# Who issues a V shift, where a q turn stands in SyncE's queue, and when the next chunk's k and q are loaded

## The chip, the cores and the metric

The kernel runs on one core of a Trainium2 chip. The metric is the device time of one execution in microseconds. The other figures come from one profiled execution; its span runs from its first to its last instruction.

## The reference, cut to what matters

Attention over 4 batches of 8 heads, 768 positions and 64 features per head: three heads (0, 2, 6) are causal, the other five see the first 4 keys and a window of 64. Then two dense layers with a leaky ReLU between.

```python
scores = (1 / sqrt(D)) * q @ k.transpose(0, 1, 3, 2)
mask   = causal (heads 0, 2, 6)  or  causal & (pos_k < 4 | rel < 64) (heads 1, 3, 4, 5, 7)
a      = softmax(where(mask, scores, -1e9))
x      = (a @ v).transpose(0, 2, 1, 3).reshape(3072, 512)
h      = x @ w_in                    # 512 -> 2048
out    = maximum(0.01 * h, h) @ w_out   # 2048 -> 512
```

## The kernel before, in words

The 3072 rows are cut into eight chunks of 384: chunk n is half c of batch b, and each batch has two chunks. All matmuls are bf16 with float32 sums. Every chunk goes through the same stations, and the kernel works at three chunks at a time. Its order is written out by hand: in the loop at L1154 round n does the first layer of chunk n (`in_slots`, letter t), the attention of chunk n + 1 (letter a), the second layer of earlier tiles (letter p) and the spreading of chunk n + 2's keys (letter e), and the string `WOVEN[n]` says letter by letter which of these pieces is issued next. Each engine then runs its own instructions strictly in the order of issue.

The stations of one chunk, with the names that the trace uses:

- **Loads**, issued by GpSimd: `load_qk` (L110, the DMA at L116) brings k into `kb` and q into `qb`, three transfers each; there is one buffer of each. `load_v` (L118, L123) brings V into `va`, three transfers. With `behind`, a one-element copy into `hold` (L121) first makes GpSimd wait for a given tile.
- **Turns**, issued by SyncE: `turn_dma` (L245, L254) transposes `kb` into `kd` and `qb` into `qd` by DMA.
- **Spread**: VectorE copies `kd` into the key tiles `kt` (L274). It can't begin before the k turn has landed.
- **V shift**: `v_shift` (L146; L150, L151) copies V, moved by 64 rows, from `va` into `vb` in two DMAs, by SyncE if no other engine is given. The window heads read `vb` as an operand of TensorE's second attention product (L336).
- **Attention** (L316): scores on TensorE (L368, L404), exponentials on ScalarE (L373, L409), masks on VectorE (L376, L378, L413), the product with V (L336). `finish` (L427) divides a pair of heads by its sums into `xs` (L438, VectorE), and `x_t` (L441) has SyncE turn `xs` into a quarter of `xt` by DMA (L443). A chunk has four such outputs, one for each pair.
- **First layer**: TensorE multiplies `w_in_bf` with `xt` (L622, one bank `ph` of two for each piece, emptied by ScalarE at L625 into `g_all`), and for some columns by a scheme with seven products in the place of eight (L710), which needs sums of `xt` from VectorE (`x_sum`, L662).
- **Second layer**: seven products for a pair of row tiles (L834), with sums of `g_all` (L793); results are stored by SyncE (L868).

What sets the order around the change is round n = 2 of the loop. It has the attention of chunk 3, whose four outputs SyncE turns. At its head it turns k and q of chunk 4 (L1160) and has GpSimd load k and q of chunk 5 (L1167); ScalarE issues the V shift of chunk 4 at the letter v (L1174). The rounds 3 and 4 end with a copy into `hold` that waits for the last quarter of the next chunk's `xt` (L1185), and behind it GpSimd loads q and V for later chunks. Round 3 begins with the turns of chunk 5 and the load of its V behind its k turn (L1162).

A DMA's queue is that of the engine that issues it. SyncE, GpSimd and ScalarE each issue in order, and an instruction that waits holds up all that stand behind it on its engine.

Of the kernel before, what the change touches and what calls it, by code (L numbers as in the profile page):

```python
# [21 lines left out]
def kernel(  # L22
# [12 lines left out]
    nc = tc.nc  # L35
# [10 lines left out]
    NCH = B * (S // CH)  # L46
# [63 lines left out]
    def load_qk(n, nms="kq"):  # L110
        b, c = ORDER[n]
        for nm in nms:
            t = rot.tile([128, 3, H, D], BF16, name=f"{nm}b", tag=f"{nm}b", bufs=1)
            raw[nm, n] = t
            for g in range(3):
                nc.gpsimd.dma_start(out=t[:, g], in_=nat[nm][b, c, :, :, g])  # L116

    def load_v(n, gs=range(3), behind=None):  # L118
        b, c = ORDER[n]
        if behind is not None:  # L120
            nc.gpsimd.tensor_copy(hold[0:1, :], behind)  # L121
        for g in gs:
            nc.gpsimd.dma_start(out=va[b][:, 3 * c + g, :, 0:D], in_=nat["v"][b, c, :, :, g])  # L123
# [3 lines left out]
    def load_sinks(b, eng=None):  # L127
        vsf[b] = vsfs[b % 2]
        (eng or nc.sync).dma_start(out=vsf[b].rearrange("(r f) d -> r f d", f=4)[:, 0], in_=v[b, :, 0:NS, :])

    def sink_values(b, eng):
        n = H - 1
        eng.tensor_tensor(
            vs[b % 2][:, 1:H, 0:D],
            vsf[b].rearrange("p (o d) -> p o d", o=1).to_broadcast([128, n, D]),
            m_sink[:, 1:H].rearrange("p (h o) -> p h o", o=1).to_broadcast([128, n, D]),
            op=ALU.mult)
# [8 lines left out]
    def v_shift(n, eng=None):  # L146
        eng = eng or nc.sync
        i, c = ORDER[n]
        lo, hi = (0, 2) if c == 0 else (2, 5)
        eng.dma_start(out=vb[i][0:64, lo:hi], in_=va[i][64:128, lo:hi, 1:H])  # L150
        eng.dma_start(out=vb[i][64:128, lo:hi], in_=va[i][0:64, lo + 1 : hi + 1, 1:H])  # L151
# [64 lines left out]
    def turn_pair(n, p, tags, engs, nms="kq"):  # L216
        b, c = ORDER[n]
        prepared.update((nm, n, p) for nm in nms)
        if n not in qx:
            qx[n] = rot.tile([128, 4, CH], BF16, name="qt", tag="qd", bufs=3)  # L220
        for nm, tag, eng in zip(nms, tags, engs):
            pt = bank(tag, [128, 4, 128], BF16)
            for g in range(3):
                nc.tensor.transpose(pt[:, g, :], raw[nm, n][:, g, 2 * p : 2 * p + 2, :], ident[:])
            if nm == "k":
                for hh in range(2):
                    move(eng[hh], kt[b % 2][hh][:, p, CH * c : CH * c + CH].rearrange("p (g t) -> p g t", g=3), pt[:, 0:3, :], hh)
            else:
                move(eng, qx[n][:, p, :].rearrange("p (g t) -> p g t", g=3), pt[:, 0:3, :])
# [15 lines left out]
    def turn_dma(n, nms="kq"):  # L245
        for nm in nms:
            dst = rot.tile([128, 3, 4, 128], BF16, name=f"{nm}d", tag=f"{nm}d", bufs=3 if nm == "q" else 2)
            if nm == "q":
                qx[n] = dst
            else:  # L250
                raw["kx", n] = dst
            thirds = [slice(j, j + 1) for j in range(1 if nm == "q" and n == 3 else 3)]
            for g in thirds if n < 4 or (nm, n) == ("k", 4) else [slice(0, 3)]:
                nc.sync.dma_start_transpose(out=dst[:, g].rearrange("p g q t -> p (g q) t"),  # L254
                                            in_=raw[nm, n][:, g].rearrange("p g h d -> p (g h d)"))
# [8 lines left out]
    def spreads(n):  # L264
        b, c = ORDER[n]

        def spread(g, hh):
            r = slice(64 * hh, 64 * hh + 64)
            o = CH * c + 128 * g
            dst, src = kt[b % 2][hh][r, :, o : o + 128], raw["kx", n][r, g]  # L270
            if n == 2 and hh:
                nc.scalar.activation(out=dst, in_=src, func=ACTF.Copy)
            else:
                nc.vector.tensor_copy(dst, src)  # L274

        order = [(g, hh) for hh in range(2) for g in range(3)] if n < 4 else [(g, hh) for g in range(3) for hh in range(2)]
        r = [lambda g=g, hh=hh: spread(g, hh) for g, hh in order]
        if c == 0:
            r += sink_keys_by(b)
        return r  # L280
# [210 lines left out]
    class First:  # L491
# [108 lines left out]
    RAMP = "XXqqqqaxYaYaaXaYakakakaaZaaZkaZsaasaaasaaataattaaatatattat"  # L600
    FIRST = "tttttttDttttL0tttt10Wt0kkk4k10k00k1k1S000k00S00aav011aSa22aa1Sa1a11a1aT1a11aa22a2a2eeaea2ee2eaa"
    WOVEN = {
        2: "aaptpIataatataatataIataItaattIaaetaeapeaatatvateaaepetteppe",
        3: "aappapapaxAppptAAaaAAtpAatAaaptaaBBAptpeeBaapaBBvetpBBpetetBe",
        4: "paappapapaxppaaApaatapatAaapAapAaAtpAaAeaeBpteeapapetaaABpeptpaBpBepatBptBpevBppppBpp",
        5: "paaxAteaAeatpaaAAtpIAaappaABApaatpBppeatBaeAIppaIeBBptpBItBtpBev",
# [139 lines left out]
    def in_tile(t0, j, tag="ph", nt=4):  # L746
        ph = bank(tag, [128, 4, 128], FP32)
        for x in range(nt):
            t = t0 + x
            for g in range(KG):  # L750
                nc.tensor.matmul(ph[:, x, :], lhsT=w_in_bf[:, g, 128 * t : 128 * t + 128],  # L751
                                 rhs=xts[0][:, j, g, :], start=(x == 0 and g == 0),
                                 stop=(g == KG - 1), skip_group_check=True)
        done[0] += nt / 3
        nc.scalar.activation(out=g_all[:, slab(0) + j, t0 : t0 + nt, :], in_=ph[:, 0:nt], func=ACTF.Prelu, alpha=0.01)
# [171 lines left out]
    def steps(k, units=None):  # L927

        r = []
        for u in units or Pair.UNITS[pairs[k].duo]:  # L930
            for half in range(2):
                def step(u=u, half=half):
                    pairs[k].unit(u, half)
                    if not half:
                        return flush()
                    pending.extend((pairs[t], i) for t, i in sums_behind(k, u))
                    flush()
                r.append(costing(0.44, step))
        return r
# [77 lines left out]
    for a in (ats4[0], ats[0]):  # L1017
# [63 lines left out]
    lists = {  # L1081
        "x": [lambda: F2.x_t("py", "v")],
        "X": [lambda j=j: in_tile(0, j) for j in range(3)],
        "Y": [lambda j=j: in_tile(4, j, nt=2) for j in range(3)],
        "Z": [lambda j=j: in_tile(6, j, nt=2) for j in range(3)],
        "q": [
            lambda: turn_pair(1, 0, ("ph",), ('v',), "q"),
            lambda: turn_pair(1, 1, ("po",), ('v',), "q"),
            lambda: turn_pair(1, 3, ("psS",), ('a',), "q"),
# [37 lines left out]
    def turn_third():  # L1127
# [3 lines left out]
    lists = {  # L1131
        "t": p1,
        "0": steps(0, ("P1", "P2", "P6", "P7", "P5", "P4", "P3")),
        "1": steps(1, ("P1", "P2", "P6", "P7", "P5", "P4", "P3")),
        "2": steps(2),
        "W": [behind_first],
        "4": [lambda: then_fourth.pop()()],
        "S": [lambda i=i: pairs[1].sum(i) for i in range(1, 5)],
        "k": keys2,
# [14 lines left out]
    for n in range(2, NCH):  # L1154
        a, extra = [], []
        if n + 2 < NCH:
            if ORDER[n + 2][1] == 0:
                load_sinks(ORDER[n + 2][0])
                sink_values(ORDER[n + 2][0], nc.gpsimd)
            turn_dma(n + 2, "q" if n == 5 else "kq")  # L1160
            if n == 3:
                load_v(n + 2, behind=raw["kx", n + 2][0:1, 0, 0, 0:1])  # L1162
            if n == 4:
                v_shift(n + 2)
            extra = spreads(n + 2)
            if n + 3 < NCH:
                load_qk(n + 3, "k" if n > 2 else "kq")  # L1167
        if n + 1 < NCH:
            a = Attention(n + 1, cross=True).slots(lag=2 if n > 3 else 3)
        lists = {"a": a, "p": outs, "x": [lambda: x_sums(n)], "e": extra, "v": [], **in_slots(n)}  # L1170
        if n in (3, 5):
            lists["v"] = [lambda: v_shift(n + 2)]
        if n == 2:
            lists["v"] = [lambda: v_shift(4, nc.scalar)]  # L1174
        if n == 4:
            lists["v"] = [lambda: turn_dma(7, "k")]
        if n in (5, 6):
            lists["I"] = in_sums_left
        if n == 2:
            lists["I"] = [lambda i=i: in_sums(0, i + 1) for i in range(4)]  # L1180
        for c in WOVEN[n]:
            lists[c].pop(0)()
        assert not any(lists[c] for c in lists if c not in "xI") and (n < 6 or not in_sums_left)
        if n in (3, 4):
            nc.gpsimd.tensor_copy(hold[0:1, :], xts[n + 1][0:1, 3, 0:1])  # L1185
            load_qk(n + 3, "q")
            load_v(n + 3)
        outs = [f for k in range(3 * n // 2, 3 * n // 2 + 1 + n % 2) for f in steps(k)]
    run(outs)

# [34 lines left out]
```

## Time and profile before

| | us |
|---|---|
| median of 3 runs | 220.78 |
| the three runs | 218.86, 220.78, 221.34 |
| the profiled execution | 219.31 |
| its span, first to last instruction | 217.4 |
| TensorE busy | 209.0 (96%) |
| VectorE busy | 165.3 (76%) |
| ScalarE busy | 150.3 (69%) |
| GpSimd busy | 72.5 (33%) |

The engines are named PE (TensorE), DVE (VectorE), ACT (ScalarE), POOL (GpSimd) and SP (SyncE). A name with a q behind it, as SPq, is the engine's issuing part: a row of it is the issue of a DMA, not its transfer. An arrow inside a name reads as "written from" (xt<-xs); behind a wait it names what ended the wait. TensorE's clock is granted in full in all 40 slices of the page.

### The profile page before, as it was taken

The numbers are of one execution on the slowest core, as the hardware profiler recorded it, in microseconds if no ns is written. First come the engines' busy times: TensorE is split into PE (matmuls) and PEld (weight loads), VectorE is DVE, ScalarE is ACT, GpSimd is POOL, SyncE is SP. The second block draws the span as 40 slices with busy tenths as digits, with TensorE's granted clock in tenths as the row PEclk, the third lists the DMA queues.
The fourth block names the chain that finished last, engine by engine and source line by source line (L and its number), as shares of the span: only waits on it lengthen the run. The fifth ranks groups of instructions, "written<-read, shape, count | busy, mean of one in ns | idle before, by whom it ended". The sixth has DMA issues, their size and how long they took to land.

```text
span 217.4 us, 6311 instructions
## 1 busy us (share of the span) xinstructions
PE 209.0 (96%) x2524; PEld 174.2 (80%) x2524; DVE 165.3 (76%) x454; ACT 150.3 (69%) x348; POOL 72.5 (33%) x91
## 2 busy tenths in 40 slices
PE   7798999999999999989999999999999999999994
PEld 5577887568898677778887978788888999999893
DVE  6683596897699477868886875799997986977653
ACT  4766985766566896658679876686677995668420
POOL 8977563019805913607219500900000000000000
PEclk9999999999999999999999999999999999999999
DMA  9999999999999999999999995996140131200222
GB/s 131 148 174 171 184 207 192 172 157 123 167 135 197 205 134 151 161 230 135 139 171 202 123 139 144 174 167 100 50 138 3 21 106 48 101 0 0 100 97 96
DMA packets 112604, 28.79 MB, mean 132 GB/s; under 512 B 102208, under 2 KB 109632, under 8 KB 112576
## 3 DMA queue, kind: packets, MB, share of 16 engines
q0 software_dynamic: 78080, 13.37, 85.4%
q1 hardware_dynamic: 33152, 14.53, 35.3%
q10 hardware_dynamic: 1344, 0.50, 1.1%
q8 instruction: 19, 0.31, 0.6%
q14 instruction: 9, 0.07, 0.1%
HBM read 27.30 MB, written 6.29 MB: 154 GB/s over the span
## 4 chain that ended last, share of the span: by engine, by line
PE 84%; DMA 7%; POOL 5%; ACTq 1%; ACT 1%; DVE 1%; issue 1%; POOLq 0%
PE py L834 18%; PE ph L622 16%; PE ph L710 9%; PE po L336 7%; PE py L813 7%; PE psS L368 5%; PE po L710 5%; DMA w_in_bf<-in_moe_w_in_dram 4%; DMA xt<-xs 3%; PE psS L404 3%; PE psS L622 2%; PE po L813 2%; PE ph L751 2%; PE po L834 2%; PE ph L813 1%; PE psS L710 1%
## 5 line engine op out<-in xcount | busy, mean ns | idle before, releaser
L622 PE MATMUL ph<-xt,w_in_bf 128*128 128x384 bf16 x224 | 44.6, 326 | 1.3 <-DMA xt<-xs 0.7
L625 ACT ACTIVATE g_all<-ph 128x384 bf16<-128x384 f32 x56 | 27.3, 490 | 16.8 <-PE ph L622 15.8
L373 ACT ACTIVATE at<-psS 128x384 bf16<-128x384 f32 x73 | 33.9, 493 | 6.5 <-PE psS L368 5.9
L622 PEld LDWEIGHTS <-w_in_bf 128*128 128x128 bf16 x256 | 23.4, 98 | 12.0 <-issue 0.8
L834 PEld LDWEIGHTS <-sum 128*128 128x128 bf16 x256 | 23.9, 98 | 2.5
L116 POOL DMA_DIRECT2D kb<-in_k_dram x21 | 18.8, 921 | 18.5 <-DMA kd<-kb 17.3
L123 POOL DMA_DIRECT2D va<-in_v_dram x24 | 21.4, 916 | 1.9 <-DMA qb<-in_q_dram 1.5
L834 PEld LDWEIGHTS <-g_all 128*128 128x128 bf16 x192 | 17.9, 98 | 2.9 <-issue 0.2
L116 POOL DMA_DIRECT2D qb<-in_q_dram x21 | 18.6, 906 | 3.8 <-DMA w_in_bf<-in_moe_w_in_dram 1.6
L368 PE MATMUL psS<-qd,kt 128*128 128x384 bf16 (+2 forms) x81 | 19.1, 290 | 0.0
L336 PE MATMUL po<-va,at 128*128 128x65 bf16 x219 | 18.5, 194 | 0.0
L409 ACT ACTIVATE ats<-psS 128x384 bf16<-128x384 f32 x33 | 15.7, 490 | 2.6 <-PE psS L404 2.4
L793 DVE TENSOR_TENSOR sum<-g_all 128x1024 bf16<-128x1024 bf16 x24 | 16.4, 683 | 1.2 <-ACT g_all L625 0.9
L336 PEld LDWEIGHTS <-at 128*128 128x128 bf16 x234 | 14.5, 98 | 3.4 <-issue 0.7
L834 PE MATMUL py<-w_sum,sum 128*128 128x256 bf16 x120 | 17.2, 272 | 0.0
L834 PE MATMUL py<-w_out_bf,sum 128*128 128x256 bf16 x120 | 16.7, 273 | 0.0
L738 ACT ACTIVATE s<-ph 128x384 f32<-128x384 f32 x27 | 13.1, 491 | 5.1 <-PE ph L710 4.5
L834 PE MATMUL py<-w_out_bf,g_all 128*128 128x256 bf16 x112 | 16.1, 273 | 0.0
L438 DVE TENSOR_TENSOR xs<-po,linv 128x384 bf16<-128x384 f32 x27 | 15.0, 557 | 0.9
L413 DVE TENSOR_TENSOR ats<-ats,m_win 128x384 bf16<-128x384 bf16 x35 | 12.2, 354 | 4.3 <-ACT ats L409 3.9
L710 PEld LDWEIGHTS <-w_in_bf 128*128 128x128 bf16 x168 | 14.1, 98 | 1.7 <-issue 1.1
L729 DVE TENSOR_TENSOR s<-po,s 128x384 f32<-128x384 f32 x21 | 11.4, 554 | 3.8 <-ACT s L738 1.8
(248 smaller groups left out, 497.5 us busy)
## 6 DMA issues: line engine op xcount, KB each, us to landing
out_dram<-o SPq DMA_DIRECT2D x23, 256.0 KB, 2.8
va<-in_v_dram POOLq DMA_DIRECT2D x24, 128.0 KB, 6.3
qb<-in_q_dram POOLq DMA_DIRECT2D x21, 128.0 KB, 7.2
kb<-in_k_dram POOLq DMA_DIRECT2D x21, 128.0 KB, 6.5
w_out_bf<-in_moe_w_out_dram POOLq DMA_DIRECT2D x4, 512.0 KB, 11.9
w_in_bf<-in_moe_w_in_dram POOLq DMA_DIRECT2D x2, 512.0 KB, 8.6
w_in_bf<-in_moe_w_in_dram POOLq DMA_DIRECT2D x4, 256.0 KB, 8.2
vb<-va SPq DMA_DIRECT2D x6, 170.6 KB, 4.0
```

The source lines that it names most:

```text
L116: nc.gpsimd.dma_start(out=t[:, g], in_=nat[nm][b, c, :, :, g])
L123: nc.gpsimd.dma_start(out=va[b][:, 3 * c + g, :, 0:D], in_=nat["v"][b, c, :, :, g])
L336: nc.tensor.matmul(o, lhsT=lhsT, rhs=rhs, start=first, stop=False, skip_group_check=True)
L368: nc.tensor.matmul(s[:, off : off + w], lhsT=kt[i][hh][:, p, 128 * kj : 128 * kj + 128], rhs=q_of(n, p, lo, CH), start=(j == 0), stop=(j = ...
L373: nc.scalar.activation(out=a[:, 0:off], in_=s[:, 0:off], func=ACTF.Exp, scale=SM)
L409: nc.scalar.activation(out=av_, in_=s[:, 0:CH].rearrange("p (j e f) -> p j e f", j=3, e=2), func=ACTF.Exp, scale=SM)
L622: nc.tensor.matmul(ph[:, 0:CH], lhsT=w_in_bf[:, g, 128 * t : 128 * t + 128], rhs=xts[n][:, g, :] if n else xts[0][:, :, g, :], start=(g == ...
L625: nc.scalar.activation(out=g_all[:, slab(n) : slab(n) + 3, t, :], in_=ph[:, 0:CH].rearrange("p (j t) -> p j t", j=3), func=ACTF.Prelu, alp ...
L710: nc.tensor.matmul(s[:, 192 * m : 192 * m + 192], lhsT=lhs[:, g, 128 * m : 128 * m + 128], rhs=rhs[:, g], start=first and m == 0 and g == ...
L793: nc.vector.tensor_tensor(self.s[i], x, y, op=op)
L813: nc.tensor.matmul(s[:, 0 : c1 - c0], lhsT=lhs[:, j, :], rhs=rhs[:, j, c0:c1], start=first and j == 0, stop=(j == NH - 1), skip_group_chec ...
L834: nc.tensor.matmul(s, lhsT=lhs[:, j, :], rhs=rhs[:, j, :], start=u in ("P1", "P2", "P5") and j == 0, stop=(j == NH - 1), skip_group_check= ...
```

## The change

Round 2 is changed in three places, and nothing is computed otherwise. The V shift of chunk 4 is issued by GpSimd at the head of the round, behind the V loads and the sink values. The turn of chunk 4's q leaves the head of the round and stands in the string at a new letter q. The loads of chunk 5's k and q leave the head too and stand at the end of the round, behind a copy into `hold` that waits for the last quarter of chunk 3's `xt`, as the later rounds have it.

```diff
-        2: "aaptpIataatataatataIataItaattIaaetaeapeaatatvateaaepetteppe",
+        2: "aaptpIataatataatataqIataItaattIaaetaeapeaatatateaaepetteppe",
...
-            turn_dma(n + 2, "q" if n == 5 else "kq")
+            turn_dma(n + 2, {2: "k", 5: "q"}.get(n, "kq"))
...
             extra = spreads(n + 2)
-            if n + 3 < NCH:
-                load_qk(n + 3, "k" if n > 2 else "kq")
+            if n == 2:
+                v_shift(4, nc.gpsimd)
+            if 2 < n < NCH - 3:
+                load_qk(n + 3, "k")
...
         if n == 2:
-            lists["v"] = [lambda: v_shift(4, nc.scalar)]
+            lists["q"] = [lambda: turn_dma(4, "q")]
...
-        if n in (3, 4):
+        if n in (2, 3, 4):
             nc.gpsimd.tensor_copy(hold[0:1, :], xts[n + 1][0:1, 3, 0:1])
-            load_qk(n + 3, "q")
-            load_v(n + 3)
+            load_qk(n + 3, "kq" if n == 2 else "q")
+            if n > 2:
+                load_v(n + 3)
```

On SyncE, in round 2: the first `kd` and `qd` are the turned k and q of chunk 4, `xt<-xs` are the four outputs of chunk 3, and the last `kd` is the k turn of chunk 5.

```order
 L129 DMA vsf_106<-in_v_dram 32x1x64
 L254 DMA_TRANSPOSE kd<-kb 128x4x128 x3
+L443 DMA_TRANSPOSE xt<-xs 128x3x128
 L254 DMA_TRANSPOSE qd<-qb 128x12x128
-L443 DMA_TRANSPOSE xt<-xs 128x3x128 x4
+L443 DMA_TRANSPOSE xt<-xs 128x3x128 x3
 L868 DMA out_dram<-o 128x512 x2
 L254 DMA_TRANSPOSE kd<-kb 128x12x128
```

The q turn now stands behind the first of the four outputs; everything below it keeps its order.

On GpSimd, from the V loads of chunk 4 (`va_81`) on: `vb` is the shifted V, `hold` the copy that waits, `kb` and `qb` are chunk 5's k and q.

```order
 L123 DMA va_81<-in_v_dram 128x8x64 x3
 L133 TENSOR_TENSOR vs_85<-vsf_106,m_sink 128x7x64
+L150 DMA vb_83<-va_81 64x2x455
+L151 DMA vb_83<-va_81 64x2x455
+L1187 COPY hold<-xt 1x1
 L116 DMA kb<-in_k_dram 128x8x64 x3
 L116 DMA qb<-in_q_dram 128x8x64 x3
```

The two halves of the V shift and a copy that waits for chunk 3's `xt` now stand ahead of the loads; behind them the order is as it was. On ScalarE the two halves are gone from between two pieces of the first layer.

## Rows read from the trace of the kernel before

**Rows 1.** The page's first part: busy us, share of the span, instructions.

```profile
PE 209.0 (96%) x2524; PEld 174.2 (80%) x2524; DVE 165.3 (76%) x454; ACT 150.3 (69%) x348; POOL 72.5 (33%) x91
```

**Rows 2.** Waits of TensorE: who, for whom, us in total, times, longest.

```profile
PE ph L622 <- DMA xt<-xs: 0.7, 1, 0.7
PE ph L622 <- ACT g_all L625: 0.6, 1, 0.6
```

**Rows 3.** TensorE's timeline: start, us, instruction, count, [idle before, releaser].

```profile
87.48 0.81 PE L622 MATMUL ph<-xt,w_in_bf 128*128 128x384 bf16 x4 [0.61 <-ACT g_all L625]
...
94.89 0.32 PE L622 MATMUL ph<-xt,w_in_bf 128*128 128x384 bf16 x1 [0.67 <-DMA xt<-xs]
...
95.94 0.19 PE L336 MATMUL po<-vb,ats 128*128 128x65 bf16 x1
...
115.57 0.19 PE L336 MATMUL po<-vb,ats 128*128 128x65 bf16 x1
```

**Rows 4.** The chain of waits from 83 to 100 us: start, us, what.

```profile
84.79 0.69 ACTq L150
...
85.58 1.31 ACTq L151
...
88.61 6.23 DMA xt<-xs
...
97.16 0.65 PE ph L622 x4
```

**Rows 5.** SyncE's timeline, 40 to 140 us: start, us of issue, DMA, count.

```profile
81.09 2.41 SPq L254 DMA_TRANSPOSE qd<-qb  x1
83.60 6.23 SPq L443 DMA_TRANSPOSE xt<-xs  x4
...
93.68 1.31 SPq L254 DMA_TRANSPOSE kd<-kb  x1
97.59 2.32 SPq L254 DMA_TRANSPOSE qd<-qb  x1
100.07 5.10 SPq L443 DMA_TRANSPOSE xt<-xs  x3
...
106.96 2.05 SPq L443 DMA_TRANSPOSE xt<-xs  x1
...
109.86 0.59 SPq L151 DMA_DIRECT2D vb<-va  x1
```

**Rows 6.** GpSimd's timeline, 30 to 140 us, columns as in rows 3.

```profile
85.23 2.70 POOL L116 DMA_DIRECT2D kb<-in_k_dram  x3 [8.59 <-DMA kd<-kb]
...
99.08 0.27 POOL L121 COPY hold<-kd 1x1 bf16<-1x1 bf16 x1 [8.22 <-DMA kd<-kb]
99.53 2.63 POOL L123 DMA_DIRECT2D va<-in_v_dram  x3 [0.18 <-issue]
...
112.96 0.26 POOL L1185 COPY hold<-xt 1x1 bf16<-1x1 bf16 x1 [8.18 <-DMA xt<-xs]
```

**Rows 7.** VectorE's timeline, 66 to 116 us, columns as in rows 3.

```profile
76.57 0.56 DVE L438 TENSOR_TENSOR xs<-po,linv 128x384 bf16<-128x384 f32 x1
...
86.05 0.56 DVE L438 TENSOR_TENSOR xs<-po,linv 128x384 bf16<-128x384 f32 x1
...
94.92 0.36 DVE L662 TENSOR_TENSOR x_sum<-xt,x_sum 128x384 bf16<-128x384 bf16 x1 [1.87 <-DMA xt<-xs]
...
105.21 0.58 DVE L274 COPY kt<-kd 64x512 bf16<-64x512 bf16 x2
...
114.25 0.36 DVE L662 TENSOR_TENSOR x_sum<-xt,x_sum 128x384 bf16<-128x384 bf16 x1
```

**Rows 8.** DMA issues, count, KB each, median us to landing: 133-134.5, 99.5-102, whole span.

```profile
xt<-xs SPq DMA_TRANSPOSE x1, 2.3
...
va<-in_v_dram POOLq DMA_DIRECT2D x3, 128.0 KB, 5.5
...
vb<-va SPq DMA_DIRECT2D x6, 170.6 KB, 4.0
```

## The prediction

> **What bounds the kernel now.** I read the page's first part, then TensorE's list of waits, then the chain of waits around those waits, then the queues that feed that stretch. The first part shows TensorE busy for 209.0 of 217.4 us [rows 1]. Its list of waits shows only two in the steady part of the kernel: 0.7 us for the transfer xt<-xs and 0.6 us for ScalarE's g_all [rows 2]. TensorE's timeline places them at 86.9 to 87.48 (0.61) and at 94.2 to 94.89 (0.67) [rows 3]; the reader should see that both stand in the pass that finishes chunk 3, and that nothing between 95 us and the last tiles holds TensorE up. Wherever TensorE doesn't wait, a faster queue is worth nothing, so the whole gain that this change can have lies in these two places, unless it makes new waits later.
>
> The chain of waits tells what each one is [rows 4]. The first: ScalarE issues the V shift of chunk 4 at 84.79 (0.69) and 85.58 (1.31), and until 86.89 it can't empty the bank that TensorE wants. The second: the transfer that turns the last of chunk 3's four outputs is issued at 88.61 and lands 6.23 us later. In SyncE's queue that transfer stands behind the q turn of chunk 4 (issued at 81.09 for 2.41) and its three sisters (from 83.60, 6.23 for all four) [rows 5]. Beside it GpSimd's loads of chunk 5's k and q run, from 85.23 on [rows 6]. VectorE waits 1.87 us for the same landing [rows 7]. A transfer of the same kind that no load stood beside took 2.3 us [rows 8], so 3.9 of the 6.2 are company.
>
> **The change part by part.** *The V shift leaves ScalarE.* Two issues, 0.69 + 1.31 us, go [rows 4], and with them the 0.61 us wait of TensorE [rows 3]. GpSimd issues them instead. It has nothing else to do there: its next work is the wait for chunk 3's outputs, and a load costs it 0.90 us (2.70 for three) [rows 6], so two shifts are about 1.8 us of an idle engine. The V data is there by about 84.8, since ScalarE's issues went out then. TensorE first reads the shifted V at 95.94 [rows 3], 94.5 if it runs 1.4 us earlier. Issued by 86.6 and with a landing as slow as the slowest row here, 6.2, the shift is there at 92.8. Cost nothing; the cover is 1.7 us.
>
> GpSimd's load issues go on at 0.90 us each while VectorE works [rows 6, 7]. The Trainium skill has a rule against this move: "SBUF — State Buffer", section "SBUF: two separate sides", says that a DMA issued by GpSimd can be held up while VectorE runs in a two-port mode, with about 620 ns becoming about 3100 ns. An estimate by that page would put some 5 us on the two issues and make TensorE wait. The 0.90 us rows don't show such a hold, so the sum goes without it.
>
> *The q turn of chunk 4 goes behind the first output.* That output is ready at 77.13 (76.57 + 0.56) [rows 7], long before the q turn leaves at 81.09, a time set by the landing of its q. So the first output goes out in a gap of the queue and the q turn isn't later. The other three then follow it from 83.60, at about 1.2 to 1.3 us each; the last must wait for its data, ready at 86.61 (86.05 + 0.56) [rows 7]. I put its issue at 86.7 instead of 88.61, 1.9 us earlier.
>
> *The loads of k and q of chunk 5 wait until all four outputs are turned.* That frees the last output from their company: it lands between 89.0 (2.3, alone) and 92.9 (6.2, as now). I take 3.2 us, near the lone row, because only the q turn and the V shift are still under way: 89.9. TensorE wants it at 94.2, or 93.6 with the first wait gone, so the 0.67 us goes too at either end.
>
> The two waits together are 1.28 us by the timeline. A group of four such matmuls shows 0.81 there and 0.65 in the chain of waits [rows 3, 4]; the ends are modelled, so each wait may be 0.16 longer. Gain 1.3 to 1.6; I take 1.4.
>
> *What the later load gives back.* GpSimd's hold copy to its next load takes 0.45 us (99.08 to 99.53) [rows 6], so chunk 5's first load moves from 85.23 to about 90.3: 5.1 later (4.2 to 8.1 by the two ends). Everything of chunk 5 hangs on it, and before it ran like this, counted from that first load: k turn issued +8.45 (93.68), q turn +12.36 (97.59) [rows 5], k turned and hold released +13.85, V loads +14.30 (99.53) [rows 6]. Without the outputs, the shift and the stores beside them I let the loads save 1 us. Then:
> - k turned at 103.1. VectorE spreads it from 105.21 on [rows 7], 103.8 when 1.4 earlier: just in time, 0.
> - q turn issued at 101.7 to 104.0, and behind it in SyncE's queue the outputs of chunk 4, which went out from 100.07. Three at 1.2 us and a store end near 108, so the last leaves about when it did before (106.96) [rows 5]. With loads beside it the whole way, 6.2 us, it lands at 113.2; before, the hold copy that waits for it ran at 112.96 [rows 6]. VectorE wants it at 114.25 [rows 7], now 112.85. Late by about 0.4 us, and VectorE's queue behind it (the masks that TensorE's next products need) with it.
> - V loads from 103.6; the third is issued 1.75 later and lands 5.5 after that [rows 8]: 110.9. The second half of the V shift follows on SyncE at 110.9 instead of 109.86 [rows 5] and lands 4.0 us later [rows 8], with loads now beside it perhaps 5: 114.9 to 115.9. TensorE reads it at 115.57 [rows 3], now 114.2. Late by 0.7 to 1.7.
>
> The last two end at the same place of TensorE's stream, so they don't add: I take 1.1 us given back, with ends of 0 (landing alone, loads quick) and about 4 (below). Later stages keep their order: TensorE comes to them only 0.3 us sooner.
>
> **Sum.** 1.4 gained, 1.1 given back: 0.3 us less. The profiled execution took 219.31 (span 217.4 and 1.9 around it), which gives 219.0; the median of the three runs is 1.5 higher, 220.78, which gives 220.5. The runs reach from 218.86 to 221.34, so I forecast the middle, 219.8, which within the noise is no change.
>
> **The rivals.**
> - *The whole gain stays.* The last output of chunk 3 lands in 2.3 us, the first load leaves at 89.5 and the loads save 2 us of their 8.45 and 12.36. Then V lands at 109.1, the second half shift at 113.2 and the last output of chunk 4 at 112.6: before they are wanted. Gain 1.3 to 1.6, time 217.7 to 219.5. For it: the lone 2.3 row. Against: chunk 4's outputs now share the chip's transfer engines with V and the next k.
> - *Slower: chunk 5's V shift comes late.* The place is TensorE's first product with the shifted V of chunk 5 at 115.57. If the landing before the hold copy takes 4.4 us (first load at 91.5) and the loads save nothing, V lands at 113.1 (91.5 + 14.30 + 1.75 + 5.5), and the shift, 5 us, at 118.1: 3.9 us late, net 2.5 slower, 221.8 to 223.3. It outweighs the gain from a first load at about 89.1 on, if the loads save nothing. For it: the chain has four links, each with a landing that company stretched to 6 us in this trace. Against: most of that company was these very loads.
> - *GpSimd issues the shift too late,* so that a wait at 95.94 takes the place of the two that go. The two issues would have to hold GpSimd or its transfers beyond 94.5, 9.7 us after the data; with 12 us the loss would be 2.3 and the net 0.9 slower, 220.2 to 221.7. The Trainium skill's rule above is the one that would do it. The 0.90 us rows speak against it.
>
> **How the numbers follow.** About 1% is what a measurement of this kernel can tell from no change: below 218.6 is faster, above 223.0 slower. Forecast 0.50, whole gain 0.27, V shift late 0.18, GpSimd late 0.05. The whole gain is at most 0.7% of 220.78, so it passes 1% only with luck of the runs: 0.12 over all. The late V shift passes it in about half its cases, and the spread of the runs adds a little: 0.12. The rest, 0.76, is within 1%. The range of 8 in 10 takes the whole gain on the low basis (217.8) and the late shift on the middle one (222.2).
>
> **What would show each step.** In the profile after: no V shift in ScalarE's queue and no wait for g_all near 87 (first step); the last output of chunk 3 issued near 86.7 and landed before 91 (second); first load of chunk 5 near 90, hold copy for its k near 103 (third); a TensorE wait of about 1 us near 114, released by vb or by VectorE behind x_sum (give-back). The forecast is wrong if TensorE has no wait there (whole gain), if that wait is over 2.5 us, or if one stands at 95.

## The result, and the profile after

The changed kernel is slower: a median of 222.98 us over 23 executions (220.49 to 226.06) against 220.38 us over 23 of the kernel before (218.34 to 221.97), ratio 1.0119, 95% interval 1.0089 to 1.0148. The forecast was 219.8. The ratios here leave out executions more than 1.5% above their kernel's fastest, which in the changed kernel are 10 of 23, the profiled one (225.64, span 223.9) among them, so the median of all executions stands beside each ratio.

The profiled execution took 6.33 us more than that of before (219.31). Its parts answer to the rows of before one by one. First the page's busy times, which hardly differ from [rows 1], and TensorE's waits (columns as in [rows 2]):

```profile
PE 212.4 (95%) x2524; PEld 175.9 (79%) x2524; DVE 166.4 (74%) x454; ACT 150.8 (67%) x348; POOL 74.2 (33%) x94
```

```profile
PE po L336 <- DVE ats L413: 3.8, 1, 3.8
...
PE po L336 <- DVE at L378: 1.0, 1, 1.0
```

The two waits of [rows 2], for xt<-xs and for g_all, are gone. Two others have come, and one of them is longer than both. TensorE's busy time grew by 3.4 us at an equal count of instructions, which a wait doesn't do; that is the clock, below. The 3.8 us wait is seen from both sides in the timelines of TensorE and VectorE (columns as in [rows 3]):

```profile
119.01 0.23 PE L336 MATMUL po<-vb,ats 128*128 128x65 bf16 x1 [3.79 <-DVE ats L413]
```

```profile
117.79 0.36 DVE L662 TENSOR_TENSOR x_sum<-xt,x_sum 128x384 bf16<-128x384 bf16 x1 [4.08 <-issue]
```

The instruction at 119.01 is the one that ran at 115.57 before [rows 3]. It waits for masks (ats) that stand in VectorE's queue behind the sums of chunk 4's xt, and the second of these sums ran at 114.25 without a wait before [rows 7]. The profile calls the releaser "issue", that is, it shows none; GpSimd's hold copy, which waits for the same tile, names it. Here is GpSimd's timeline, to be read against [rows 6]:

```profile
86.96 0.67 POOL L150 DMA_DIRECT2D vb<-va  x1 [8.17 <-DMA va<-in_v_dram]
88.29 0.60 POOL L151 DMA_DIRECT2D vb<-va  x1 [0.67 <-DMA va<-in_v_dram]
92.22 0.18 POOL L1187 COPY hold<-xt 1x1 bf16<-1x1 bf16 x1 [3.32 <-DMA xt<-xs]
92.84 2.67 POOL L116 DMA_DIRECT2D kb<-in_k_dram  x3 [0.44 <-issue]
...
103.99 0.20 POOL L121 COPY hold<-kd 1x1 bf16<-1x1 bf16 x1 [5.86 <-DMA kd<-kb]
104.44 2.73 POOL L123 DMA_DIRECT2D va<-in_v_dram  x3 [0.26 <-issue]
107.15 2.68 POOL L116 DMA_DIRECT2D kb<-in_k_dram  x3
117.83 0.36 POOL L1187 COPY hold<-xt 1x1 bf16<-1x1 bf16 x1 [8.01 <-DMA xt<-xs]
```

The two shifts of chunk 4 at the top landed in 3.4 us (DMA issues from 86 to 89 us):

```profile
vb<-va POOLq DMA_DIRECT2D x2, 113.8 KB, 3.4
```

At the bottom, chunk 4's last output lands just before 117.83 (112.96 before), and the k loads of chunk 6, from 107.15 on, now lie right across it. SyncE's queue, against [rows 5]:

```profile
82.47 3.21 SPq L254 DMA_TRANSPOSE qd<-qb  x1
85.78 5.20 SPq L443 DMA_TRANSPOSE xt<-xs  x3
...
101.72 1.63 SPq L254 DMA_TRANSPOSE qd<-qb  x1
103.51 4.27 SPq L443 DMA_TRANSPOSE xt<-xs  x3
108.31 0.33 SPq L868 DMA_DIRECT2D out_dram<-o  x1
108.75 1.27 SPq L443 DMA_TRANSPOSE xt<-xs  x1
111.38 0.64 SPq L150 DMA_DIRECT2D vb<-va  x1
112.39 0.59 SPq L151 DMA_DIRECT2D vb<-va  x1
```

The last output of chunk 4 leaves at 108.75 instead of 106.96 and takes 9 us instead of 5.9; the two halves of chunk 5's V shift leave at 111.38 and 112.39 instead of 109.86 for the second, and their landing took 6.3 us in the median of the two (DMA issues from 111 to 119 us: count, KB each, us to landing):

```profile
vb<-va SPq DMA_DIRECT2D x2, 170.6 KB, 6.3
```

So the second half, which took 6.0, is there at about 118.4, and TensorE's first product with it would have waited nearly as long if the sums had been in time.

What follows the wait was not in the forecast at all. TensorE stands still, and when it resumes its clock is granted at half (1.2 instead of 2.4 GHz). The windows show it; the columns are the stretch, its length, busy time of PE, PEld, DVE, ACT and POOL with counts, the granted clock, the DMA share and GB/s:

```profile
110.00:116.00 6.00, 5.22 (x64) 4.21 (x61) 3.21 (x8) 5.08 (x12) 0.00 (x0) 1.00 2.02 178
116.00:118.00 2.00, 0.00 (x0) 0.00 (x0) 0.21 (x1) 0.00 (x0) 0.17 (x1) 1.00 0.98 209
118.00:120.00 2.00, 0.99 (x11) 0.78 (x12) 1.56 (x5) 0.12 (x1) 1.48 (x3) 0.52 0.65 129
120.00:122.00 2.00, 2.00 (x12) 1.06 (x10) 0.75 (x2) 1.05 (x3) 2.00 (x3) 0.50 1.16 132
122.00:124.00 2.00, 2.00 (x11) 1.20 (x10) 0.23 (x1) 0.68 (x2) 2.00 (x4) 0.50 2.41 149
124.00:126.00 2.00, 2.00 (x26) 1.74 (x25) 0.79 (x2) 1.25 (x3) 2.00 (x3) 0.77 2.42 150
```

Four matmuls with 384 columns advance the chain of waits by 1.28 us there instead of 0.65, twice as long (start, us, what; before the wait and behind it):

```profile
100.38 0.65 PE ph L622 x4
...
120.00 1.28 PE ph L622 x4
```

The sum for this execution: 1.28 us of waits gone, 0.96 for the keys of chunk 4 at 85.5 (L378; runs of several kernels show such a wait, below), 3.79 at 119.01. That makes 3.47 us late, and the instruction at 119.01 stands 3.44 behind its place of before. The half clock from there to 125 us costs 0.48 + 1.0 + 1.0 + 0.46 = 2.9 (busy time by the share of the clock that is missing, window by window): 6.4 in all, of 6.33.

Over all executions the clock is about half of the loss. One minus an execution's mean granted clock, times its span, is on average 1.7 us in the 23 of the changed kernel and 0.3 us in 29 of the kernel before, those run beside the repeated change below; the mean clock is below 0.996 in 17 of the 23 and in 3 of the 29. The figure is a little high, since it also counts low clock under which TensorE stands still, as between 118 and 119 us above.

### The profile page after: what moved, and what is told of

Its sections match the earlier page's. It is cut to its first block, busy times and chain, and to the rows that moved or that the text cites. A ratio compares the mean times of both kernels' runs of the same rounds, so it can differ in the third digit from the quotient of the medians.

```text
span 223.9 us, 6316 instructions
## 1 busy us (share of the span) xinstructions
PE 212.4 (95%) x2524; PEld 175.9 (79%) x2524; DVE 166.4 (74%) x454; ACT 150.8 (67%) x348; POOL 74.2 (33%) x94
## 4 chain that ended last, share of the span: by engine, by line
PE 54%; DMA 28%; issue 8%; POOL 5%; DVE 2%; SPq 1%; ACT 0%; POOLq 0%
PE py L834 18%; PE ph L710 9%; DMA kd<-kb 8%; PE ph L622 8%; DMA w_in_bf<-in_moe_w_in_dram 7%; DMA w_out_bf<-in_moe_w_out_dram 6%; DMA kb<-in_k_dram 5%; PE po L710 5%; PE po L336 5%; PE psS L368 3%; DMA xt<-xs 2%; POOL va L123 2%; PE po L834 2%; PE psS L404 1%; PE psS L710 1%
## 5 line engine op out<-in xcount | busy, mean ns | idle before, releaser
L622 PE MATMUL ph<-xt,w_in_bf 128*128 128x384 bf16 x224 | 45.7, 333 | 0.0
L622 PEld LDWEIGHTS <-w_in_bf 128*128 128x128 bf16 x256 | 23.8, 99 | 11.7 <-issue 0.7
L368 PE MATMUL psS<-qd,kt 128*128 128x384 bf16 (+2 forms) x81 | 19.7, 298 | 0.0
L710 PEld LDWEIGHTS <-w_in_bf 128*128 128x128 bf16 x168 | 14.3, 99 | 1.1 <-issue 0.5
L336 PEld LDWEIGHTS <-ats 128*128 128x128 bf16 x210 | 10.2, 98 | 5.6 <-DVE ats L413 4.1
```

The source lines that it names most:

```text
L336: nc.tensor.matmul(o, lhsT=lhsT, rhs=rhs, start=first, stop=False, skip_group_check=True)
L368: nc.tensor.matmul(s[:, off : off + w], lhsT=kt[i][hh][:, p, 128 * kj : 128 * kj + 128], rhs=q_of(n, p, lo, CH), start=(j == 0), stop=(j = ...
L622: nc.tensor.matmul(ph[:, 0:CH], lhsT=w_in_bf[:, g, 128 * t : 128 * t + 128], rhs=xts[n][:, g, :] if n else xts[0][:, :, g, :], start=(g == ...
L710: nc.tensor.matmul(s[:, 192 * m : 192 * m + 192], lhsT=lhs[:, g, 128 * m : 128 * m + 128], rhs=rhs[:, g], start=first and m == 0 and g == ...
```

## The experiments

The theory (A): the moved loads alone make the loss, by the chain first load, k turn, V loads, V shift, with SyncE's outputs beside it; the other two parts cost nothing. Against it stood that the loss comes from GpSimd's issue of the shift or from the q turn in the middle of the outputs, and that one link of the chain (the k loads of chunk 6, or the V loads that wait for the k turn) makes it alone.

**The change again.**

> The changed kernel once more, for a second profile. Theory A (the late loads of chunk 5 push its V, its q turn and the k of chunk 6 beside chunk 4's four outputs, and VectorE waits for the last of them at x_sum): slower than before by 0.8 to 1.5%, one wait of TensorE of 1 to 5 us between 113 and 119 us behind a VectorE wait at x_sum (L662), and a granted clock under 1.00 in the stretch after it. Theory B (the V shift on GpSimd or the q turn behind the first output is what costs): the waits stand between 85 and 97 us.

Measured: median 223.68 of 12 (219.30 to 226.34) against 219.94 of the kernel before. The ratio, 0.9988 (0.9924 to 1.0053), rests on only 4 of the 12 and says little: 9 of the 12 show a mean clock below 0.996, with a median of 224.15, and the other three lie near 219.4. So the price isn't paid in every execution. Its profile took 224.8 us; TensorE waits here for the V shift itself: 2.1 us at 117.79, the longer of the two waits of this row (the other, 1.6 us at 62.57, stands ahead of the change). The chain of waits (start, us, what) shows the last three links, behind a first load at 91.20:

```profile
PE po L336 <- DMA vb<-va: 3.7, 2, 2.1
```

```profile
96.97 4.81 DMA kd<-kb
...
104.09 7.43 DMA va<-in_v_dram
111.54 6.12 DMA vb<-va
```

VectorE's wait for the last output was 1.58 us, that for V 2.1: which of the two ends last differs between the two profiles of this kernel, the place doesn't.

**The third part undone.** The loads go back to the head of the round, now behind GpSimd's V shift; the other two parts stay.

```diff
-            if 2 < n < NCH - 3:
-                load_qk(n + 3, "k")
+            if n < NCH - 3:
+                load_qk(n + 3, "kq" if n == 2 else "k")
...
-        if n in (2, 3, 4):
+        if n in (3, 4):
...
```

> The change without its third part: chunk 5's k and q are loaded at the head of the round again, behind the V shift on GpSimd. Theory A: the wait near 114 us is gone, ScalarE's wait near 87 us too, the wait for the last output of chunk 3 near 94 us is back in part; 0 to 0.8% faster than before. Theory B: still about 1.2% slower than before.

Measured: ratio 1.0017 (0.9969 to 1.0065), medians 221.05 and 219.94. The first load left at 87.52 in its profile and the clock stayed at 1.00. The loss of 1.2% is gone, within the interval; the gain that was expected didn't show. Nor did the waits go quite as expected: at 117.61 TensorE still waits 1.0 us for vb, and the wait for the last output of chunk 3 is back in full (0.8 us).

**The third part alone.** ScalarE issues the V shift and the q turn stays at the head, as before; only the loads move.

```diff
-            if n + 3 < NCH:
-                load_qk(n + 3, "k" if n > 2 else "kq")
+            if 2 < n < NCH - 3:
+                load_qk(n + 3, "k")
...
-        if n in (3, 4):
+        if n in (2, 3, 4):
...
```

> The third part of the change alone: V shift on ScalarE and q turn ahead of all outputs, as before; chunk 5's k and q loaded once all four outputs of chunk 3 are turned. Theory A: as slow as the whole change or slower, 1.0 to 2.0% over before, with the wait at x_sum near 114 us. Theory B: within 0.5% of before or faster.

Measured: ratio 1.0104 (1.0066 to 1.0143), medians 222.61 and 219.94: the whole loss by this part alone. Its profile has the same wait, nearly the same landing (8.3 us) and a clock as low (0.69 and 0.50 in the two windows after 118 us). VectorE waits 3.82 us for the last output. TensorE's list, GpSimd's timeline and the chain:

```profile
PE po L336 <- DVE ats L413: 3.5, 1, 3.5
```

```profile
92.18 2.70 POOL L116 DMA_DIRECT2D kb<-in_k_dram  x3 [0.42 <-issue]
```

```profile
108.58 8.26 DMA xt<-xs
```

This run also parts the two effects of the move. The last output of chunk 3, free of company, landed 2.4 us after its issue instead of 6.2, and neither wait of [rows 2] is left, though ScalarE still issues the shift. So the move of the loads alone takes away the wait for xt, the part of the forecast's saving that came from company. For ScalarE's wait one profile says less, since that wait goes by V's landing (below).

**The first part alone,** ahead of the loads at the head, run twice.

```diff
+            if n == 2:
+                v_shift(4, nc.gpsimd)
             if n + 3 < NCH:
...
-        if n == 2:
-            lists["v"] = [lambda: v_shift(4, nc.scalar)]
...
```

> The first part alone: the V shift of chunk 4 is issued by GpSimd, ahead of the loads of chunk 5's k and q, which so start behind the landing of V; the q turn as before. Theory A: ScalarE's wait near 87 us goes (0.6 us), the wait near 94 us stays, the loads start 1 to 2.5 us later than before and a wait of 0 to 2 us near 114 us appears: between 0.4% faster and 0.6% slower than before. Theory B (issuing from GpSimd costs): 1% slower or more, with TensorE waiting for vb near 95 us.

> The V shift by GpSimd alone, a second time, on the question whether its 0.6% was luck. If the part is worth ScalarE's wait of 0.6 us and more: a ratio of 0.992 to 0.998. If not: 0.999 or above. In the profile no wait of TensorE for g_all near 87 us.

Measured: ratios 0.9938 (0.9896 to 0.9981) and 0.9946 (0.9901 to 0.9991). The medians of all executions are 219.2 against 220.4 in the first set, but 220.14 against 220.18 in the second, so a gain of half a per cent is likely and its size open. By these ratios it is the fastest version tried, and the first is better than the range that was expected. In the first profile the first load left at 89.35, and TensorE, made late by a wait of 2.6 us at 87.93 for the keys of chunk 4, waited for nothing of chunk 5. The second profile is its slowest execution (224.18) and shows the chain at work in a kernel that loads at the head: V landed late, GpSimd's shift waited for it, and the loads stood behind the shift. The chain of waits:

```profile
74.58 13.27 DMA va<-in_v_dram
...
88.53 0.66 POOL vb L150
...
90.18 1.77 POOL kb L116 x2
91.95 6.45 DMA kb<-in_k_dram
...
98.46 5.14 DMA kd<-kb
...
105.90 6.91 DMA va<-in_v_dram
...
112.83 7.14 DMA vb<-va
```

TensorE waits 2.5 us for vb in it. No load was moved on purpose here; a first load at 90.2 was enough in this execution.

**The second part alone.**

```diff
-        2: "aaptpIataatataatataIataItaattIaaetaeapeaatatvateaaepetteppe",
+        2: "aaptpIataatataatataqIataItaattIaaetaeapeaatatvateaaepetteppe",
...
```

> The second part alone: the q turn of chunk 4 behind the first output of chunk 3; V shift on ScalarE and loads at the head as before. Theory A: within 0.4% of before; the last output is issued up to 2 us earlier, but lands beside the loads as before, so the wait near 94 us is shorter and not gone. Theory B: 1% slower.

Measured: ratio 0.9992 (0.9956 to 1.0027), medians 220.3 and 220.4: nothing. Its profile shows what ScalarE's issue costs when V lands late. The chain of waits:

```profile
73.38 13.86 DMA va<-in_v_dram
...
87.25 0.60 ACTq L151
...
87.90 0.50 ACT g_all L625
...
88.44 0.81 PE ph L622 x4
```

ScalarE waits for V, and TensorE waits 2.0 us for the bank that ScalarE would have emptied, instead of 0.6 as in [rows 2]. So the first wait has no fixed size: it goes by V's landing. GpSimd's queue takes that wait off TensorE, which fits the gain of the first part.

**The shift on SyncE.** The first two parts with another engine: v_shift(4) without an engine, at the old letter v, the q turn at q, the loads at the head.

> The q turn behind the first output, loads at the head as before, and the V shift issued by SyncE between the third and the last output. Theory A: the loads start as early as before, so no wait near 114 us; ScalarE's wait near 87 us is gone; the last output is issued about 1.3 us later than without the shift in front: 0 to 0.6% faster than before.

Measured: ratio 0.9982 (0.993 to 1.0034), medians 221.39 and 220.4. No difference shown. Its profile keeps a wait of 0.6 us for xt and has none for chunk 5; its wait of 1.1 for vb stands at 61.81, ahead of the change.

**The k of chunk 6 later,** behind the hold on chunk 4's outputs, so that nothing but V stands beside them.

```diff
-            if 2 < n < NCH - 3:
+            if 3 < n < NCH - 3:
...
-            load_qk(n + 3, "kq" if n == 2 else "q")
+            load_qk(n + 3, "kq" if n < 4 else "q")
```

> The whole change, and the k of chunk 6 is loaded behind the copy that waits for chunk 4's last output, so that three transfers fewer run beside these outputs. Theory A: the last output of chunk 4 lands 2 to 4 us earlier than in the changed kernel, TensorE's wait near 114 us is under 1.5 us, and the time is between 0.7% faster and 0.3% slower than before. If V and the late turn of chunk 5's q alone make the outputs late, and not chunk 6's k: still 0.8% slower or more.

Measured: ratio 1.0184 (1.0124 to 1.0244), medians 224.49 and 219.94: worse. Yet the wait at chunk 4's sums is gone. The issue at 108.33 landed 3.8 us later (9 in the changed kernel), so by this pair of profiles chunk 6's k was the company that stretched it. The landing came earlier, by more than theory A expected, and the wait near 114 us went, but not the time. The wait is one link further on, in TensorE's list, SyncE's queue and the chain:

```profile
PE po L336 <- DVE at L378: 3.3, 1, 3.3
```

```profile
119.75 1.73 SPq L254 DMA_TRANSPOSE kd<-kb  x1
```

```profile
119.75 8.00 DMA kd<-kb
127.77 0.28 DVE kt L274
```

**V of chunk 5 right behind its q,** no longer behind its k turn, to cut a link out of the chain.

```diff
-            if n == 3:
-                load_v(n + 2, behind=raw["kx", n + 2][0:1, 0, 0, 0:1])
...
-            if n > 2:
-                load_v(n + 3)
+            load_v(n + 3)
```

> The whole change, and chunk 5's V is loaded right behind its q, no longer behind its k turn. If chunk 5's late V (and its shift) is what TensorE waits for: vb and the last output of chunk 4 land 2 us earlier than in the changed kernel and the time is within 0.5% of before. If chunk 6's k beside the last output of chunk 4 is what makes it late: the wait at x_sum stays, 0.7% slower than before or more.

Measured: ratio 1.0116 (1.0065 to 1.0168), medians 222.76 and 220.18: no better than the change. V's loads now stand beside the k turn, which took 9.2 us instead of 4.2 in the changed kernel. Neither expectation named the place of this wait: VectorE spreads the keys late, and its sums for TensorE stand behind that; at x_sum nothing waits. TensorE's list, and the chain:

```profile
PE po L710 <- DVE s L729: 3.2, 1, 3.2
```

```profile
99.50 9.19 DMA kd<-kb
108.71 0.28 DVE kt L274
```

**Only q of chunk 5 behind the hold,** its k at the head.

```diff
-            if 2 < n < NCH - 3:
+            if n < NCH - 3:
...
-            load_qk(n + 3, "kq" if n == 2 else "q")
+            load_qk(n + 3, "q")
```

> The whole change, but only the q of chunk 5 waits for the four outputs; its k is loaded at the head behind the V shift. Theory A: chunk 5's k turn is issued near 95 us as with the loads at the head, its V loads and its last output's company move back with it, so the wait near 114 us is at most half that of the changed kernel: between 0.2% faster and 0.6% slower than before.

Measured: the ratio, 0.9999 (0.991 to 1.0089), rests on 2 of 12 executions; the median of all is 225.34 (218.88 to 228.81) against 220.4, the worst of all versions, with a mean clock below 0.996 in 11 of 12. The profiled execution (221.03) is one of those two and shows a 2.5 us wait for chunk 4's keys and none for chunk 5. It is within what was expected, the other ten are not. By the sum used above the clock takes 2.8 us on average over the 12; where their waits stand is open.

**The hold on the second output,** so that the loads leave earlier.

```diff
-            nc.gpsimd.tensor_copy(hold[0:1, :], xts[n + 1][0:1, 3, 0:1])
+            nc.gpsimd.tensor_copy(hold[0:1, :], xts[n + 1][0:1, 1 if n == 2 else 3, 0:1])
```

> The whole change, but the copy that releases chunk 5's loads waits for the second of chunk 3's outputs in the place of the last, so the loads start about 1.5 us earlier, near 90 us. Theory A (the time of the loads decides): between loads at the head (1.002) and the whole change (1.012), about 1.006. If the waiting for the outputs itself costs, whatever the time of release: as slow as the whole change.

Measured: ratio 1.0103 (1.0061 to 1.0146), medians 222.08 and 220.18. That is as slow as the whole change, and not the 1.006 expected if the time of the loads decides, although they left near 90 as meant. In its profile the wait for the second output ended at 89.83:

```profile
90.45 2.67 POOL L116 DMA_DIRECT2D kb<-in_k_dram  x3 [0.26 <-issue]
```

```profile
117.16 0.22 PE L336 MATMUL po<-vb,ats 128*128 128x65 bf16 x1 [2.58 <-DMA vb<-va]
```

Put together: with the first load at 85.2 (before) or 87.5 no loss shows; at 90.5 the ratio is 1.010, at 92.2 1.010, at 92.8 1.012 (each time from the one profile of its kernel). With the loads at the head single executions wait too when V lands late: 1.0 us with a first load at 87.5, 2.5 with one at 90.2. So the third part makes the loss, and first loads some 5 us later use up the slack of a chain of four transfers (k loads, k turn, V loads, V shift). That each further microsecond is paid isn't shown: from 90.5 to 92.8 the ratios don't part. A cost of the waiting itself isn't excluded by the held runs alone; against it stand the 2.5 us paid without such a hold. And ten of twelve executions are slower than the changed kernel's median when chunk 5's k is at the head and only its q is held, which this account doesn't explain.

## Why the prediction was wrong, step by step

The gain came: both waits of TensorE are gone. The step that failed is the third, "What the later load gives back", and in size: 1.1 us was taken, and the profiled execution waited 3.8 us at that place, with 2.9 of half clock behind it that no term held. By the prediction's own signs that is a wait "over 2.5 us". The second step missed its times as well: the last output of chunk 3 was to be issued near 86.7 and landed before 91, and was issued at 89.50 and landed by 92.2.

| step | forecast | profile after |
|---|---|---|
| shift issued by GpSimd | out by 86.6, costs nothing | 86.96 and 88.29, costs nothing |
| last output of chunk 3: issue | 86.7 | 89.50, the third of the row at 85.78 |
| its landing | 3.2 us | 2.7 at most (hold copy at 92.22) |
| the two waits | gone, 1.3 to 1.6 us | gone |
| first load of chunk 5 | 90.3 | 92.84 |
| what the loads save on the way to the V loads | 1 us | 2.7 us (11.6 instead of 14.30) |
| V loads | 103.6 | 104.44 |
| last output of chunk 4: issue | 106.96 | 108.75 |
| its landing | 6.2 us | 9.0 us |
| second half of the V shift: issue | 110.9 | 112.39 |
| its landing | 4 to 5 us | about 6 us |
| TensorE's wait | 1.1 us | 3.8 us |

- *The V shift leaves ScalarE:* right. The rule of the Trainium skill that the prediction weighed ("SBUF — State Buffer", "SBUF: two separate sides") did not show: the two issues took 0.67 and 0.60 us, with VectorE busy for 0.62 and 0.57 of them, and landed in 3.4 us. Whether VectorE ran in a two-port mode then, no row tells. What the working missed is that the shift waits for V, and that this landing varies: V wasn't there by 84.8 but by 87 to 88.
- *The q turn behind the first output:* harmless, but the issue at 86.7 was wrong by nearly 3 us. The q turn left at 82.47 instead of 81.09 and took 3.21 us instead of 2.41, and the three outputs behind it 5.20 together, so the change of place gained nothing at the last output (it left at 87.85 with the q turn alone moved, 88.61 before, 89.07 with the loads alone moved). Why the issues took longer here isn't shown. The delay goes into the first load, 92.84 instead of 90.3.
- *The last output of chunk 4:* the working itself had "three at 1.2 us and a store end near 108" and then put the last at 106.96 all the same. The queue was the limit: the data was ready at 106.7 (106.10 + 0.56 on VectorE), the third output's issue lasted until 107.78, a store ahead of the last left at 108.31, and the issue came at 108.75.
- *Its landing:* the 6.2 us of [rows 4] was taken as the worst that company does. It was an instance. With chunk 5's V (from 104.44) and chunk 6's k (from 107.15) issued just in front of it, the same transfer took 9.0, 8.3 in the run of the third part alone, and 3.8 when chunk 6's k was kept away.
- *The rival "chunk 5's V shift comes late"* is what came, at its place. That its 3.9 us is so near the 3.8 measured is luck: its first load was 1.3 us too early, its loads saved nothing instead of 2.7 us, its shift landed in 5 us instead of 6, and what ended last in this profile was the last output of chunk 4, the shift being there at about 118.4. Its condition, first load from about 89.1 on if the loads save nothing, was met with 3.7 us to spare, 1.0 if the saving is taken off. It was held back by "most of that company was these very loads": true of chunk 3's outputs, but the moved loads put other loads beside chunk 4's outputs.
- *The clock* was in no sum. Of the 2.6 us between the medians about 1.4 is clock (1.7 less 0.3, above), so without it the loss is 1.2, a time of about 221.6, just under that rival's range of 221.8 to 223.3. The median of 222.98 lies in this range only with the clock, which the rival didn't count.
- *Smaller slips in the working:* "each with a landing that company stretched to 6 us" doesn't hold for the V shift, whose row is 4.0 [rows 8]. The late shift on the middle basis is 222.6 (220.1 + 2.5), not 222.2, and the 112.6 of the first rival has no working. None of this would have put 222.98 in the range.

## What to carry to other kernels

A load that is moved later to free one transfer of its company moves a whole chain of transfers behind it: count that chain's slack to its last reader, and reprice every landing in the company that it has after the move, not before it. An early prefetch that seems only to disturb may be what gives the next stage its slack; taking one link out of the chain (later k, earlier V) moved the wait to another link each time. A wait on TensorE is also dearer than its length where the clock falls behind it, so a change that trades two short waits for one long one should be counted with that price.

## What was not expected of the hardware

- After a standstill of 3.8 us TensorE's granted clock was about 0.5 for some 6 us, then 1.00 again. The same followed the waits in the profiles of the repeated change (2.1 us; 0.64 and 0.51), of the loads alone (3.5 us; 0.69 and 0.50) and of the hold on the second output (2.6 us; 0.62 and 0.53). It also followed waits that ended between 85 and 89 us and have nothing to do with chunk 5: 2.0 us in the profile of the second part alone (0.50 from 90 to 92 us), 2.6 in the first profile of the first part alone (0.50 from 90 to 92), 2.5 where only q is held (0.50 from 88 to 90). It did not follow the waits of 3.3 and 3.2 us in the profiles of the later k and the earlier V, nor the 2.5 us in the second run of the first part, where the clock stayed at 1.00. Length alone doesn't decide it, and what does was not tried.
- How often it happens goes with the loads: a mean clock below 0.996 stands in 17 of 23 executions of the changed kernel and 7 of 12 with the loads alone moved, and in one execution of each run with the third part undone, the first part alone (twice) and the second alone.
- The landing of one kind of transposing transfer (xt<-xs) went from 2.4 to 9.0 us by what stood beside it; its issue took from 1.2 to 2.3 us in the same profiles.
- V of chunk 4 took 13.3 and 13.9 us to land in the chains of two profiles, and the k turn of chunk 4 9.4 us in that of the changed kernel, issued ahead of everything that the change touches. The k turn gives the kernels here a wait of 0 to 2.6 us between 84 and 88 us (L378), which differs between executions; how much of their spread it makes was not tried.
